# Super-blocks of 16,384 keys, one V buffer with 64 KB rows, and V products 512 columns wide in a decode-attention kernel

## The chip, the cores and the metric

The kernel runs on one core of a Trainium2 chip. The core's engines work side by side, each through its own list of instructions: TensorE (PE; its weight loads are listed apart as PEld), VectorE (DVE), ScalarE (ACT), GpSimd (POOL) and SyncE (SP, which here only issues transfers). Sixteen DMA engines move data from device memory into on-chip memory. The metric is the device time of one execution in microseconds (us).

## The reference

The result mixes two branches for a single token of width 448: `g * a + (1 - g) * b`, where g is a sigmoid of a dot product. Branch b is a small mixer MLP. Branch a, nearly all of the work, is attention of one query token over a cache of 65,536 keys, with 16 query heads that share 8 key/value heads of 256 columns:

```python
B, Sq, D = 1, 1, 448
Hq, Hkv, Sk, Dh = 16, 8, 65536, 256
q = (x @ wq).reshape(B, Sq, Hq, Dh).transpose(0, 2, 1, 3)
k = jnp.repeat(k_cache, Hq // Hkv, axis=1)
v = jnp.repeat(v_cache, Hq // Hkv, axis=1)
scores = jnp.einsum("bhqd,bhkd->bhqk", q, k) * (Dh ** -0.5)
p = softmax(scores)
o = jnp.einsum("bhqk,bhkd->bhqd", p, v)
a = o.transpose(0, 2, 1, 3).reshape(B, Sq, Hq * Dh) @ wo
```

All data are bf16. K and V are 268 MB each, and each byte is used once, for two query heads.

## The kernel before, in words

The keys are cut into 64 blocks of 8,192 (`BLK`), eight for each key/value head; n counts them. Key p·64 + j of a block lies on partition p, so one block of K or of V is a load of 4 MB with one run of 32 KB for each of 128 partitions. K has two buffers (`k_tiles`, chosen by n % 2) and V two (`v_tiles`), 128 KB per partition together.

For each block, in the order in which the loop from L442 writes it:

- 16 groups. Each group is `transposes`: eight PE transposes of 128x128 of K (L316) into PSUM and one DVE copy of 128x1024 back (L321). After every second group PE does four score products (L331), two groups behind.
- In the first block only: the issue of the load of wo (L461) and `mixer_tail`, 14 PE products (L280) that read `gel`, the mixer's activations. `gel` lies in `v_tiles[0]`, and the query weights wq lie in `v_tiles[1]`, until V needs the place.
- On SP's list: the load of V of block n (L138), then the load of K of block n + 2 (L132). The first waits until the products that read that V buffer are done, and in block 0 until `mixer_tail` has read `gel`. The second waits until the transposes of block n are done. SP executes its list strictly in order, so an issue behind a waiting one waits too.
- `max_rows`, `max_heads`, `softmax` (L355 to L396): the row maximum, its spreading over partitions by two small PE steps, the exponential on ACT, a DVE transpose of p.
- The V products of the block before (`pv`, L346): 64 products with 2 weight columns (the two query heads) and 256 moving columns, spread over four column groups of PE; the first half stands between the two PE steps of the softmax, the second half behind them. `accumulate` (L400) folds the sum into `acc`.

The V products thus run one block behind their scores. At the end of each head come `denominators`, `head_out` and `project` (L408, L420, L433). After the last block the V products of that block stand alone, then the last head's output. The last V load is cut in five pieces (`LAST`), the first K load in four (`QUARTERS`).

All instructions of one engine are chained in program order by `seq`; nothing reorders them.

Of the kernel before, what the change touches and what calls it, by code (L numbers as in the profile page):

```python
# [20 lines left out]

BLK = 8192
KP = BLK // 128


NJ = 16
NI = KP // NJ
ROWS = REP * NI


@with_exitstack
def kernel(
# [29 lines left out]
    def seq(ins):  # L62
# [17 lines left out]

    k_tiles = [kvpool.tile([128, KP, DH], BF16, name=f"kn{i}") for i in range(2)]
    v_tiles = [kvpool.tile([128, KP, DH], BF16, name=f"vt{i}") for i in range(2)]
    kT_tiles = [work.tile([128, 2, NJ, 128], BF16, name=f"kT{i}") for i in range(2)]
    p_tiles = [work.tile([128, 512], BF16, name=f"p_sb{i}") for i in range(2)]
    pT_tiles = [work.tile([128, 512], BF16, name=f"pT{i}") for i in range(2)]
    wo_sb = const.tile([128, HQ, 2, D], BF16)

    tps = [psum.tile([128, 1024], BF16, name=f"tps{i}") for i in range(3)]
    sc_ps = [psum.tile([128, 512], FP32, name=f"sc_ps{i}") for i in range(2)]
    pv_ps = psum.tile([128, DH], FP32, name="pv_ps")  # L90
    sm_ps = psum.tile([128, 512], FP32, name="sm_ps")
# [11 lines left out]
    DM = 384  # L103
    wq_m = v_tiles[1][:, 0:48, :].rearrange("p a b -> p (a b)").rearrange(
        "p (k n) -> p k n", k=3
    )
    wq_t = v_tiles[1][:, 48:56, :].rearrange("p a b -> p (a b)")

# [18 lines left out]

    def load_k(n, pieces):
        g, b = divmod(n, NB)
        src = A_k_cache[0, g, b * BLK:(b + 1) * BLK, :].rearrange("(p j) d -> p j d", j=KP)  # L130
        for j0, j1 in pieces:
            seq(nc.sync.dma_start(out=k_tiles[n % 2][:, j0:j1, :], in_=src[:, j0:j1, :]))  # L132

    def load_v(n, pieces):
        g, b = divmod(n, NB)
        src = A_v_cache[0, g, b * BLK:(b + 1) * BLK, :].rearrange("(p j) d -> p j d", j=KP)
        for j0, j1 in pieces:
            seq(nc.sync.dma_start(out=v_tiles[n % 2][:, j0:j1, :], in_=src[:, j0:j1, :]))  # L138

    WHOLE = [(0, KP)]  # L140
    QUARTERS = [(i * NJ, (i + 1) * NJ) for i in range(NI)]
    LAST = [(0, 32), (32, 48), (48, 56), (56, 60), (60, 64)]

    load_k(0, QUARTERS)
    load_k(1, WHOLE)


# [11 lines left out]
    ))  # L159
    fst = const.tile([128, REP], FP32)  # L160
    seq(nc.vector.tensor_reduce(
        out=fst[:],
        in_=ident_f[:].rearrange("p (a i r) -> p r a i", a=4, r=REP)[:, :, :, 0:1],
        op=ALU.add, axis=AXIS.XY,
    ))
    nval = const.tile([128, REP], FP32)
# [22 lines left out]
    for h in range(HQ):  # L189
# [29 lines left out]
    b1f = const.tile([128, NF], FP32)  # L219
    gel = v_tiles[0][:].rearrange("p a b -> p (a b)")[:, 0:NF * D].rearrange(  # L220
        "p (b n) -> p b n", b=NF
# [70 lines left out]

    acc = work.tile([128, DH], FP32)
    lsum = work.tile([128, 1], FP32)
# [4 lines left out]
    nb_tiles = [work.tile([128, 1], FP32, name=f"nb{i}") for i in range(2)]  # L299
    den_tiles = [work.tile([128, 1], FP32, name=f"den{i}") for i in range(2)]  # L300
    al_tiles = [work.tile([128, 1], FP32, name=f"al{i}") for i in range(3)]
    rden = work.tile([128, 1], FP32)
    esc = work.tile([128, REP], FP32)
    oT = work.tile([128, 2, REP], BF16)
# [5 lines left out]
    def transposes(n, i, c, half):  # L310

        kT = kT_tiles[(n * NI + i) % 2]
        tp = tps[state["t"] % 3]
        state["t"] += 1
        for jj in range(8):
            seq(nc.tensor.transpose(  # L316
                tp[:, jj * 128:(jj + 1) * 128],
                k_tiles[n % 2][:, i * NJ + half * 8 + jj, c * 128:(c + 1) * 128],
                ident[:, :],
            ))  # L320
        seq(nc.vector.tensor_copy(  # L321
            out=kT[:, c, half * 8:(half + 1) * 8, :],
            in_=tp[:, :].rearrange("p (j n) -> p j n", j=8),
        ))

    def scores(n, i, c):
        kT = kT_tiles[(n * NI + i) % 2]
# [12 lines left out]
    def pv(n, j0, j1):  # L340
        pT = pT_tiles[n % 2]
        vt = v_tiles[n % 2]
        for j in range(j0, j1):
            i, jj = divmod(j, NJ)
            grp = j % 4
            seq(nc.tensor.matmul(  # L346
                pv_ps[32 * grp:32 * grp + REP, :],
                lhsT=pT[:, 32 * jj + REP * i:32 * jj + REP * (i + 1)],
                rhs=vt[:, j, :],
                start=(j < 4),  # L350
                stop=(j >= KP - 4),
                tile_position=(0, 32 * grp),
            ))
# [20 lines left out]
    def softmax(n):  # L374
        b = n % NB
        nb, nb_old = nb_tiles[n % 2], nb_tiles[(n + 1) % 2]
        den, al = den_tiles[n % 2], al_tiles[n % 3]
# [8 lines left out]
        seq(nc.scalar.activation(  # L386
            out=p_tiles[n % 2][:, :], in_=sc_ps[n % 2][:, :], func=ACT.Exp, scale=scale,
            bias=nb[:, 0:1], accum_out=den[:, 0:1],
        ))
        seq(nc.vector.transpose(out=pT_tiles[n % 2][:, :], in_=p_tiles[n % 2][:, :]))  # L390
        if b > 0:
            seq(nc.vector.scalar_tensor_tensor(  # L392
                out=lsum[:], in0=lsum[:], scalar=al[:, 0:1], in1=den[:], op0=ALU.mult, op1=ALU.add
            ))
        else:
            seq(nc.vector.tensor_copy(out=lsum[:], in_=den[:]))  # L396

    def accumulate(n):
        if n % NB > 0:
            seq(nc.vector.scalar_tensor_tensor(  # L400
                out=acc[:], in0=acc[:], scalar=al_tiles[n % 3][:, 0:1], in1=pv_ps[:, :],
                op0=ALU.mult, op1=ALU.add,
            ))
        else:
            seq(nc.vector.tensor_copy(out=acc[:], in_=pv_ps[:, :]))

# [10 lines left out]
    def head_out():  # L417

        for c in range(2):
            seq(nc.tensor.matmul(  # L420
                hd_ps[:, 464 + REP * c:464 + REP * (c + 1)],
                lhsT=acc[:].rearrange("p (d c) -> p c d", c=2)[:, c, :], rhs=esc[:],
                start=True, stop=True,
            ))
# [16 lines left out]

    for n in range(NBLK):  # L442
        groups = [(i, c, half) for i in range(NI) for c in range(2) for half in range(2)]
        due = []
        head_done = n >= 2 and (n - 1) % NB == 0
        for t, (i, c, half) in enumerate(groups):
            transposes(n, i, c, half)
            if due and due[0][0] <= t:
                scores(n, *due.pop(0)[1])
            if half == 1:  # L450
                due.append((t + 2, (i, c)))
            if head_done:
                if t == 1:
                    head_out()
                if t == 3:
                    project((n - 1) // NB - 1)
        while due:
            scores(n, *due.pop(0)[1])

        if n == 0:  # L460
# [3 lines left out]
            mixer_tail()  # L464
        load_v(n, WHOLE if n < NBLK - 1 else LAST)
        if n + 2 < NBLK:
            load_k(n + 2, WHOLE)
        max_rows(n)
        if n > 0:
            pv(n - 1, 0, 32)  # L470
        max_heads(n)
        if n > 0:
            pv(n - 1, 32, KP)
        softmax(n)
        if n > 0:
            accumulate(n - 1)
        if n % NB == NB - 1 or (n == NBLK - 1):
            denominators()
    n = NBLK - 1
    pv(n, 0, KP)  # L480
    accumulate(n)
    head_out()
    project(HKV - 1)
    fin = const.tile([1, D], FP32)
# [35 lines left out]
```

## Time and profile before

| | us |
|---|---|
| median of 3 runs | 1303.34 |
| lowest and highest run | 1302.52, 1304.71 |
| span of the profiled execution (first to last instruction) | 1300.9 |
| PE busy, DVE busy, ACT busy in it | 970.5, 835.7, 73.5 |
| DVE copies of transposed K (L321), 1,024 of them | 666.9 |
| K transposes on PE (L316), 8,192 | 629.1 |
| score products (L331), 2,048 | 212.9 |
| V products (L346), 4,096 | 135.2 |
| PE idle until a K load has landed | 203.6 |

For the profiled execution only the span is recorded; it stands 2.4 us below the median of the runs. The span is read from the profile's page, which also gives the busy share of each engine and of the DMA engines in 40 equal slices of 32.5 us. The DMA queues moved 546.40 MB at a mean of 420 GB/s. A row of a group names the line, the engine, the operation and its tiles, the count, the busy time and the mean duration of one instruction in ns, and then the idle time ahead of it with what ended it. Busy times of PE overlap where four column groups work at once.

### The profile page before, as it was taken

To read this page: it belongs to the slowest core of one execution; us is meant where nothing else is said; L and a number is where in the kernel's file an instruction comes from. 1 tells how busy PE (TensorE), PEld (TensorE's weight loads), DVE (VectorE), ACT (ScalarE), POOL (GpSimd) and SP (SyncE) were. 2 spreads that over 40 slices of the span, in tenths; PEclk is the share of its full clock that TensorE was granted. 3 is DMA by queue.
4 is the path that set the end of the run, shared out by engine and by line. 5 is a ranking of instruction groups with operands and counts; after the bars stand their busy time and mean duration, and the time that the engine had idled before them with its cause. 6 is when DMAs were issued, how large, how long until landed. Compare 5 with 4: busy or idle time off the path is not lost.

```text
span 1300.9 us, 32264 instructions
## 1 busy us (share of the span) xinstructions
PE 970.5 (75%) x14750; PEld 723.8 (56%) x14750; DVE 835.7 (64%) x1599; ACT 73.5 (6%) x203; POOL 2.4 (0%) x7
## 2 busy tenths in 40 slices
PE   3876877777886877867768768778678787777786
PEld 2565655555664655655545546556556555555564
DVE  3665766766765757756757667567567566666675
ACT  4000000000000000000000000000000000000000
POOL 0000000000000000000000000000000000000000
PEclk9888888888988879889989898899888988988888
DMA  8999999999999999999999999999999999999995
GB/s 337 410 431 431 427 431 428 430 429 431 430 424 431 431 431 429 428 428 432 430 425 431 432 428 429 429 417 430 431 423 425 425 428 426 423 425 427 428 423 221
DMA packets 22830, 546.40 MB, mean 420 GB/s; under 512 B 2980, under 2 KB 5158, under 8 KB 5670
## 3 DMA queue, kind: packets, MB, share of 16 engines
q1 hardware_dynamic: 21810, 544.22, 98.1%
q8 instruction: 115, 1.88, 0.6%
q10 hardware_dynamic: 884, 0.13, 0.1%
q14 instruction: 21, 0.17, 0.0%
HBM read 544.34 MB, written 0.00 MB: 418 GB/s over the span
## 4 chain that ended last, share of the span: by engine, by line
DMA 66%; PE 31%; DVE 1%; ACT 1%; issue 0%; ACTq 0%; DVEq 0%
DMA kn<-in_A_k_cache_dram 66%; PE tps L316 24%; PE sc_ps L331 5%; DMA xt<-in_A_x_dram 1%; ACT vt L245 1%; PE hd_ps L433 1%; PE hd_ps L420 0%; PE pv_ps L346 0%; DVE kT L321 0%; PE hd_ps L280 0%; DVE pT L390 0%; DVE rmax L356 0%; ACT L256 0%; ACT p_sb L386 0%; ACTq L515 0%
## 5 line engine op out<-in xcount | busy, mean ns | idle before, releaser
L321 DVE COPY kT<-tps 128x1024 bf16<-128x1024 bf16 x1024 | 666.9, 686 | 248.0 <-PE tps L316 233.8
L316 PE MATMUL tps<-ident,kn 128*128 128x128 bf16 x8192 | 629.1, 240 | 208.7 <-DMA kn<-in_A_k_cache_dram 203.6
L316 PEld LDWEIGHTS <-kn 128*128 128x128 bf16 x8192 | 546.7, 109 | 322.4 <-DMA kn<-in_A_k_cache_dram 220.8
L331 PE MATMUL sc_ps<-kT,qpad 128*32 128x512 bf16 x2048 | 212.9, 406 | 38.6 <-DVE kT L321 38.0
L346 PE MATMUL pv_ps<-vt,pT 128*2 128x256 bf16 x4096 | 135.2, 274 | 0.0
L331 PEld LDWEIGHTS <-qpad 128*32 128x32 bf16 x2048 | 53.0, 93 | 109.3 <-issue 60.6
L346 PEld LDWEIGHTS <-pT 128*2 128x2 bf16 x4096 | 85.8, 83 | 20.3
L390 DVE STREAM_TRANSPOSE pT<-p_sb 128x512 bf16<-128x512 bf16 x64 | 45.5, 711 | 64.8 <-ACT p_sb L386 64.8
L383 ACT ACTIVATE al<-nb,nb 128x1 f32<-128x1 f32 x56 | 16.5, 295 | 1053.6 <-DVE nb L378 1053.6
L356 DVE TENSOR_REDUCE rmax<-sc_ps 128x1 f32<-128x512 f32 x64 | 44.2, 691 | 31.5 <-PE sc_ps L331 31.5
L359 PE MATMUL sm_ps<-ident_f,rmax 128*1 128x128 f32 x64 | 17.3, 270 | 52.5 <-DVE rmax L356 52.5
L386 ACT ACTIVATE p_sb<-sc_ps,nb 128x512 bf16<-128x512 f32 x64 | 42.9, 670 | 150.5 <-DVE nb L378 150.5
L378 DVE CUSTOM_DVE_ANT_0 junk<-sm_ps,nval 128x2 f32<-128x2 f32 x64 | 10.2, 159 | 59.8 <-PE sm_ps L370 59.8
L359 PEld LDWEIGHTS sm_ps<-ident_f,rmax 128*1 128x1 f32 x64 | 5.1, 79 | 71.7 <-DVE rmax L356 71.7
L400 DVE SCALAR_TENSOR_TENSOR acc<-acc,al,pv_ps 128x256 f32<-128x256 f32 x56 | 26.5, 473 | 1.5 <-PE pv_ps L346 1.5
L370 PEld LDWEIGHTS sm_ps<-mrun,ones_row 1*128 1x128 f32 x128 | 18.7, 183 | 14.6 <-issue 14.1
L370 PE MATMUL sm_ps<-mrun,ones_row 1*128 1x2 f32 x128 | 24.2, 257 | 0.3 <-DVE mrun L363 0.3
L363 DVE TENSOR_REDUCE mnew<-sm_ps 1x2 f32<-1x32 f32 x56 | 10.0, 178 | 20.3 <-PE sm_ps L359 20.3
L194 PE MATMUL hd_ps<-xm,vt 128*128 128x1 bf16 x96 | 3.6, 165 | 12.2 <-DMA xm<-in_A_x_dram 12.2
L386 ACT ACTIVATION_READ_ACCUMULATOR p_sb<-sc_ps,nb 128x1 f32 x64 | 12.2, 191 | 0.0
L194 PEld LDWEIGHTS <-vt 128*128 128x128 bf16 x96 | 3.6, 104 | 12.1 <-DMA vt<-in_A_wq_dram 11.8
L392 DVE SCALAR_TENSOR_TENSOR lsum<-lsum,al,den 128x1 f32<-128x1 f32 x56 | 9.9, 177 | 0.0
(66 smaller groups left out, 96.9 us busy)
## 6 DMA issues: line engine op xcount, KB each, us to landing
kn<-in_A_k_cache_dram SPq DMA_DIRECT2D x63, 4096.0 KB, 27.7
vt<-in_A_v_cache_dram SPq DMA_DIRECT2D x63, 4096.0 KB, 32.4
kn<-in_A_k_cache_dram SPq DMA_DIRECT2D x4, 1024.0 KB, 11.8
wo_sb<-in_A_wo_dram SPq DMA_DIRECT2D x1, 3584.0 KB
vt<-in_A_wq_dram SPq DMA_DIRECT2D x1, 3072.0 KB
vt<-in_A_v_cache_dram SPq DMA_DIRECT2D x1, 2048.0 KB, 20.8
vt<-in_A_v_cache_dram SPq DMA_DIRECT2D x1, 1024.0 KB
vt<-in_A_wq_dram SPq DMA_DIRECT2D x2, 256.0 KB, 3.9
```

Of the source, the lines that this page charges most:

```text
L245: seq(nc.scalar.activation(out=gel[:, b, :], in_=h_bc[:], func=ACT.Gelu_apprx_tanh, scale=w1f[:, b:b + 1], bias=b1f[:, b:b + 1],))
L316: seq(nc.tensor.transpose(tp[:, jj * 128:(jj + 1) * 128], k_tiles[n % 2][:, i * NJ + half * 8 + jj, c * 128:(c + 1) * 128], ident[:, :],))
L321: seq(nc.vector.tensor_copy(out=kT[:, c, half * 8:(half + 1) * 8, :], in_=tp[:, :].rearrange("p (j n) -> p j n", j=8),))
L331: seq(nc.tensor.matmul(S[32 * a:32 * (a + 1), :], lhsT=qpad[:, c, g, i, :], rhs=kT[:, c, :, 32 * a:32 * (a + 1)], start=(i == 0 and c == 0 ...
L346: seq(nc.tensor.matmul(pv_ps[32 * grp:32 * grp + REP, :], lhsT=pT[:, 32 * jj + REP * i:32 * jj + REP * (i + 1)], rhs=vt[:, j, :], start=(j ...
L356: seq(nc.vector.tensor_reduce(out=rmax[:], in_=sc_ps[n % 2][:, :], op=ALU.max, axis=AXIS.X))
L359: seq(nc.tensor.transpose(sm_ps[0:1, 0:128], rmax[:, 0:1], ident_f[:, :]))
L370: seq(nc.tensor.matmul(sm_ps[:, 128:128 + REP], lhsT=ones_row[0:1, :], rhs=mrun[0:1, :], start=True, stop=True))
L383: seq(nc.scalar.activation(out=al[:], in_=nb_old[:], func=ACT.Exp, scale=-1.0, bias=nb[:, 0:1]))
L386: seq(nc.scalar.activation(out=p_tiles[n % 2][:, :], in_=sc_ps[n % 2][:, :], func=ACT.Exp, scale=scale, bias=nb[:, 0:1], accum_out=den[:, ...
L390: seq(nc.vector.transpose(out=pT_tiles[n % 2][:, :], in_=p_tiles[n % 2][:, :]))
L400: seq(nc.vector.scalar_tensor_tensor(out=acc[:], in0=acc[:], scalar=al_tiles[n % 3][:, 0:1], in1=pv_ps[:, :], op0=ALU.mult, op1=ALU.add,))
```

## The change

`BLK` becomes 16,384, so a head has four super-blocks and the kernel 32. Key p·128 + j of a super-block lies on partition p. K is loaded in two halves of 4 MB (64 of the 128 key columns each, 32 KB runs at a pitch of 64 KB), one into each K buffer. V is one load of 8 MB in rows of 64 KB into a single buffer `vt`, which takes the place of the two V buffers; wq and `gel` lie in that buffer before. A super-block has 32 groups and one softmax over a 128x512 tile of scores, in which 16 of each 32 rows now hold scores and 8 did before. The V products take two groups of columns at once: 4 weight columns, 512 moving columns, 64 products for a super-block; only the diagonal half of each result is used, and `fst` and `esc` pick it in `head_out`, which has twice as many products. The V products are no longer one block behind: they stand behind the softmax of their own super-block. SP's list is V(n), then the first and the second K half of n + 1. The first K load is cut in two pieces; the last V load is cut in five.

The core of the diff:

```diff
-BLK = 8192
-KP = BLK // 128
+BLK = 16384
+VP = BLK // 128
+KP = VP // 2
-NI = KP // NJ
+NI = VP // NJ
-    v_tiles = [kvpool.tile([128, KP, DH], BF16, name=f"vt{i}") for i in range(2)]
+    vt = kvpool.tile([128, VP, DH], BF16, name="vt")
-    pv_ps = psum.tile([128, DH], FP32, name="pv_ps")
+    pv_ps = psum.tile([128, 2, DH], FP32, name="pv_ps")
-    wq_m = v_tiles[1][:, 0:48, :].rearrange("p a b -> p (a b)").rearrange(
+    wq_m = vt[:, 0:48, :].rearrange("p a b -> p (a b)").rearrange(
-    wq_t = v_tiles[1][:, 48:56, :].rearrange("p a b -> p (a b)")
+    wq_t = vt[:, 48:56, :].rearrange("p a b -> p (a b)")
+    def load_v(n):
+        seq(nc.sync.dma_start(out=vt[:, :, :], in_=v_src(n)))
+    def load_v_last(n):
+        for j0, j1 in ((0, 64), (64, 96)):
+            seq(nc.sync.dma_start(out=vt[:, j0:j1, :], in_=v_src(n)[:, j0:j1, :]))
+        for j0, j1 in ((0, 8), (8, 12), (12, 16)):
...
-    load_k(0, QUARTERS)
-    load_k(1, WHOLE)
+    load_k(0, 0, [(0, 32), (32, KP)])
+    load_k(0, 1, WHOLE)
-    gel = v_tiles[0][:].rearrange("p a b -> p (a b)")[:, 0:NF * D].rearrange(
+    gel = vt[:, 56:128, :].rearrange("p a b -> p (a b)")[:, 0:NF * D].rearrange(
+    def pv(ip, j0, j1):
+        for jj in range(j0, j1):
+            grp = jj % 4
             seq(nc.tensor.matmul(
+                pv_ps[32 * grp:32 * grp + 2 * REP, :, :],
+                lhsT=pT[:, 32 * jj + 2 * REP * ip:32 * jj + 2 * REP * (ip + 1)],
+                rhs=vt[:, 2 * ip * NJ:2 * (ip + 1) * NJ, :].rearrange(
+                    "p (i j) d -> p i j d", i=2
+                )[:, :, jj, :],
...
         if n == 0:
...
             mixer_tail()
-        load_v(n, WHOLE if n < NBLK - 1 else LAST)
-        if n + 2 < NBLK:
-            load_k(n + 2, WHOLE)
+        if n < NBLK - 1:
+            load_v(n)
+            load_k(n + 1, 0, WHOLE)
+            load_k(n + 1, 1, WHOLE)
+        else:
+            load_v_last(n)
         max_rows(n)
-        if n > 0:
-            pv(n - 1, 0, 32)
         max_heads(n)
-        if n > 0:
-            pv(n - 1, 32, KP)
         softmax(n)
-        if n > 0:
-            accumulate(n - 1)
-        if n % NB == NB - 1 or (n == NBLK - 1):
+        if n % NB == NB - 1:
             denominators()
-    n = NBLK - 1
-    pv(n, 0, KP)
-    accumulate(n)
-    head_out()
-    project(HKV - 1)
+        for ip in range(NI // 2):
+            pv(ip, 0, NJ)
+        accumulate(n)
+        if n % NB == NB - 1:
+            head_out()
+            project(n // NB)
```

More of the change, by code (lines that the diff above doesn't have):

```diff
@@ L18 @@
 REP = HQ // HKV
-BLK = 8192
-KP = BLK // 128
+BLK = 16384
+VP = BLK // 128
+KP = VP // 2
 NJ = 16
-NI = KP // NJ
-ROWS = REP * NI
+NI = VP // NJ
 @with_exitstack
@@ L81 @@
     k_tiles = [kvpool.tile([128, KP, DH], BF16, name=f"kn{i}") for i in range(2)]
-    v_tiles = [kvpool.tile([128, KP, DH], BF16, name=f"vt{i}") for i in range(2)]
+    vt = kvpool.tile([128, VP, DH], BF16, name="vt")
     kT_tiles = [work.tile([128, 2, NJ, 128], BF16, name=f"kT{i}") for i in range(2)]
-    p_tiles = [work.tile([128, 512], BF16, name=f"p_sb{i}") for i in range(2)]
-    pT_tiles = [work.tile([128, 512], BF16, name=f"pT{i}") for i in range(2)]
+    p_sb = work.tile([128, 512], BF16)
+    pT = work.tile([128, 512], BF16)
     wo_sb = const.tile([128, HQ, 2, D], BF16)
@@ L126, with load_k, v_src @@
         seq(nc.scalar.dma_start(out=b2b[:], in_=B_b2.rearrange("(o n) -> o n", o=1)))
-    def load_k(n, pieces):
+    def load_k(n, h, pieces):
         g, b = divmod(n, NB)
-        src = A_k_cache[0, g, b * BLK:(b + 1) * BLK, :].rearrange("(p j) d -> p j d", j=KP)
+        src = A_k_cache[0, g, b * BLK:(b + 1) * BLK, :].rearrange("(p j) d -> p j d", j=VP)
         for j0, j1 in pieces:
-            seq(nc.sync.dma_start(out=k_tiles[n % 2][:, j0:j1, :], in_=src[:, j0:j1, :]))
-    def load_v(n, pieces):
+            seq(nc.sync.dma_start(
+                out=k_tiles[h][:, j0:j1, :], in_=src[:, h * KP + j0:h * KP + j1, :]
+            ))
+    def v_src(n):
         g, b = divmod(n, NB)
-        src = A_v_cache[0, g, b * BLK:(b + 1) * BLK, :].rearrange("(p j) d -> p j d", j=KP)
-        for j0, j1 in pieces:
-            seq(nc.sync.dma_start(out=v_tiles[n % 2][:, j0:j1, :], in_=src[:, j0:j1, :]))
+        return A_v_cache[0, g, b * BLK:(b + 1) * BLK, :].rearrange("(p j) d -> p j d", j=VP)
+    def load_v(n):
[4 more added lines that the diff above has]
+        for j0, j1 in ((0, 8), (8, 12), (12, 16)):
+            seq(nc.sync.dma_start(
+                out=vt[:, 96:128, :].rearrange("p (i j) d -> p i j d", i=2)[:, :, j0:j1, :],
+                in_=v_src(n)[:, 96:128, :].rearrange("p (i j) d -> p i j d", i=2)[:, :, j0:j1, :],
+            ))
     WHOLE = [(0, KP)]
-    QUARTERS = [(i * NJ, (i + 1) * NJ) for i in range(NI)]
-    LAST = [(0, 32), (32, 48), (48, 56), (56, 60), (60, 64)]
-    load_k(0, QUARTERS)
-    load_k(1, WHOLE)
+    load_k(0, 0, [(0, 32), (32, KP)])
+    load_k(0, 1, WHOLE)
     ident = const.tile([128, 128], BF16)
@@ L159 @@
     ))
[L160 to L165, printed above, removed]
+    fst = const.tile([128, 2, REP], FP32)
+    for e in range(2):
+        seq(nc.vector.tensor_reduce(
+            out=fst[:, e, :],
+            in_=ident_f[:].rearrange("p (a i r) -> p r a i", a=4, r=REP)[:, :, :, e:e + 1],
+            op=ALU.add, axis=AXIS.XY,
+        ))
     nval = const.tile([128, REP], FP32)
@@ L290, in mixer_tail @@
         seq(nc.vector.tensor_tensor(out=rest[:], in0=y_sb[:], in1=rest[:], op=ALU.subtract))
-    acc = work.tile([128, DH], FP32)
+    acc = work.tile([128, 2, DH], FP32)
     lsum = work.tile([128, 1], FP32)
@@ L299 @@
     nb_tiles = [work.tile([128, 1], FP32, name=f"nb{i}") for i in range(2)]
-    den_tiles = [work.tile([128, 1], FP32, name=f"den{i}") for i in range(2)]
-    al_tiles = [work.tile([128, 1], FP32, name=f"al{i}") for i in range(3)]
+    den = work.tile([128, 1], FP32)
+    al = work.tile([128, 1], FP32)
     rden = work.tile([128, 1], FP32)
-    esc = work.tile([128, REP], FP32)
+    esc = work.tile([128, 2, REP], FP32)
     oT = work.tile([128, 2, REP], BF16)
@@ L310, in transposes @@
     def transposes(n, i, c, half):
-        kT = kT_tiles[(n * NI + i) % 2]
+        kT = kT_tiles[i % 2]
         tp = tps[state["t"] % 3]
@@ L317, in transposes @@
                 tp[:, jj * 128:(jj + 1) * 128],
-                k_tiles[n % 2][:, i * NJ + half * 8 + jj, c * 128:(c + 1) * 128],
+                k_tiles[i // (NI // 2)][:, i % (NI // 2) * NJ + half * 8 + jj, c * 128:(c + 1) * 128],
                 ident[:, :],
@@ L326, in scores @@
     def scores(n, i, c):
-        kT = kT_tiles[(n * NI + i) % 2]
+        kT = kT_tiles[i % 2]
         S = sc_ps[n % 2]
@@ L338, in scores @@
             ))
[L340 to L351, printed above, removed]
+    def pv(ip, j0, j1):
+        for jj in range(j0, j1):
+            grp = jj % 4
+            seq(nc.tensor.matmul(
+                pv_ps[32 * grp:32 * grp + 2 * REP, :, :],
[3 more added lines that the diff above has]
+                )[:, :, jj, :],
+                start=(ip == 0 and jj < 4),
+                stop=(ip == NI // 2 - 1 and jj >= NJ - 4),
                 tile_position=(0, 32 * grp),
@@ L376, in softmax @@
         nb, nb_old = nb_tiles[n % 2], nb_tiles[(n + 1) % 2]
-        den, al = den_tiles[n % 2], al_tiles[n % 3]
         seq(nc.vector.tensor_tensor_reduce(
@@ L386, in softmax @@
         seq(nc.scalar.activation(
-            out=p_tiles[n % 2][:, :], in_=sc_ps[n % 2][:, :], func=ACT.Exp, scale=scale,
+            out=p_sb[:, :], in_=sc_ps[n % 2][:, :], func=ACT.Exp, scale=scale,
             bias=nb[:, 0:1], accum_out=den[:, 0:1],
         ))
-        seq(nc.vector.transpose(out=pT_tiles[n % 2][:, :], in_=p_tiles[n % 2][:, :]))
+        seq(nc.vector.transpose(out=pT[:, :], in_=p_sb[:, :]))
         if b > 0:
@@ L400, in accumulate @@
             seq(nc.vector.scalar_tensor_tensor(
-                out=acc[:], in0=acc[:], scalar=al_tiles[n % 3][:, 0:1], in1=pv_ps[:, :],
+                out=acc[:], in0=acc[:], scalar=al[:, 0:1], in1=pv_ps[:, :, :],
                 op0=ALU.mult, op1=ALU.add,
@@ L404, in accumulate @@
         else:
-            seq(nc.vector.tensor_copy(out=acc[:], in_=pv_ps[:, :]))
+            seq(nc.vector.tensor_copy(out=acc[:], in_=pv_ps[:, :, :]))
     def denominators():
@@ L419, in head_out @@
         for c in range(2):
[L420 to L424, printed above, removed]
+            for e in range(2):
+                seq(nc.tensor.matmul(
+                    hd_ps[:, 464 + REP * c:464 + REP * (c + 1)],
+                    lhsT=acc[:, e, :].rearrange("p (d c) -> p c d", c=2)[:, c, :],
+                    rhs=esc[:, e, :],
+                    start=(e == 0), stop=(e == 1),
+                ))
         seq(nc.vector.tensor_copy(
@@ L442 @@
     for n in range(NBLK):
+        due = []
         groups = [(i, c, half) for i in range(NI) for c in range(2) for half in range(2)]
-        due = []
-        head_done = n >= 2 and (n - 1) % NB == 0
         for t, (i, c, half) in enumerate(groups):
@@ L451 @@
                 due.append((t + 2, (i, c)))
-            if head_done:
-                if t == 1:
-                    head_out()
-                if t == 3:
-                    project((n - 1) // NB - 1)
         while due:
@@ L464 @@
             mixer_tail()
-        load_v(n, WHOLE if n < NBLK - 1 else LAST)
-        if n + 2 < NBLK:
-            load_k(n + 2, WHOLE)
+        if n < NBLK - 1:
[4 more added lines that the diff above has]
+            load_v_last(n)
         max_rows(n)
-        if n > 0:
-            pv(n - 1, 0, 32)
         max_heads(n)
-        if n > 0:
-            pv(n - 1, 32, KP)
         softmax(n)
-        if n > 0:
-            accumulate(n - 1)
-        if n % NB == NB - 1 or (n == NBLK - 1):
+        if n % NB == NB - 1:
             denominators()
-    n = NBLK - 1
-    pv(n, 0, KP)
-    accumulate(n)
-    head_out()
-    project(HKV - 1)
+        for ip in range(NI // 2):
[4 more added lines that the diff above has]
+            project(n // NB)
     fin = const.tile([1, D], FP32)
```

## The prediction

> **What bounds the kernel now.** I first read the rows of DMA traffic on the page, then its queues.
>
> ```profile
> DMA  8999999999999999999999999999999999999995
> GB/s 337 410 431 431 427 431 428 430 429 431 430 424 431 431 431 429 428 428 432 430 425 431 432 428 429 429 417 430 431 423 425 425 428 426 423 425 427 428 423 221
> ...
> q1 hardware_dynamic: 21810, 544.22, 98.1%
> q8 instruction: 115, 1.88, 0.6%
> ```
>
> From the third slice to the last but one the 16 engines are never idle, at 417 to 432 GB/s, and SP's queue q1 (the loads) fills 98.1% of 16 engines' span. The load stream sets the time: only what changes its rate, stops it, or lies before its first or behind its last byte can move the end. Next, whether the queue ever runs short, by the DMA issues, and whether the compute engines keep up, by the groups.
>
> ```profile
> kn<-in_A_k_cache_dram SPq DMA_DIRECT2D x63, 4096.0 KB, 27.7
> vt<-in_A_v_cache_dram SPq DMA_DIRECT2D x63, 4096.0 KB, 32.4
> L321 DVE COPY kT<-tps 128x1024 bf16<-128x1024 bf16 x1024 | 666.9, 686 | 248.0 <-PE tps L316 233.8
> L316 PE MATMUL tps<-ident,kn 128*128 128x128 bf16 x8192 | 629.1, 240 | 208.7 <-DMA kn<-in_A_k_cache_dram 203.6
> ```
>
> A 4 MB load takes 4.194 MB / 429 GB/s = 9.8 us and lands 27.7 us after its issue, so some 18 us of work stand ahead of it. PE waits 203.6 us in all for K: compute has slack. Then the two ends of the span. The start, by the timeline:
>
> ```profile
> 17.12 0.61 SPq L461 DMA_DIRECT2D wo_sb<-in_A_wo_dram  x1
> ...
> 40.80 2.81 PE L280 MATMUL hd_ps<-vt,w2b 128*1 128x448 bf16 x14
> 43.64 0.34 SPq L138 DMA_DIRECT2D vt<-in_A_v_cache_dram  x1
> ```
>
> SP issues everything up to wo by 17.7 us and then stands until `mixer_tail` (L280) has read `gel`; V(0) goes out at 43.64. The end, by the busy time of stages (stage; length; PE, PEld, DVE, ACT, POOL; clock; DMA share; GB/s):
>
> ```profile
> 1275.00:1280.00 5.00, 5.00 (x47) 4.33 (x45) 3.35 (x5) 0.00 (x0) 0.00 (x0) 0.50 1.01 424
> 1280.00:1285.00 5.00, 5.00 (x77) 3.62 (x75) 4.57 (x8) 0.00 (x0) 0.00 (x0) 0.99 0.54 230
> 1285.00:1290.00 5.00, 3.60 (x71) 2.32 (x68) 3.69 (x8) 0.00 (x0) 0.00 (x0) 1.00 0.49 200
> 1290.00:1295.00 5.00, 3.83 (x112) 2.76 (x100) 1.77 (x7) 0.96 (x3) 0.00 (x0) 1.00 0.21 78
> ```
>
> At 1280 half of the DMA engines are through; the other half, some 12 us behind, finish near 1292. And by the chain that ended last, merged in order of time:
>
> ```profile
> 1274.27 3.60 PE tps L316 x32
> ...
> 1293.05 1.95 PE pv_ps L346 x64
> 1295.02 0.49 DVE acc L400
> ```
>
> The last K block lands at 1274.2; from there to 1300.9, 26.7 us, are compute: 14.0 of transposes and scores, 4.8 of softmax and denominators, 1.95 of V products, the rest head output and the store.
>
> **Part 1, the start: one V buffer, with `gel` in it.** V(0) is still behind `mixer_tail`, but block 0 now has 32 groups, not 16. The second half follows without a pause (its K, the old block 1, was there: PE began on that at 46.94 without a wait for it). In steady rows of the timeline PE starts a new pair of groups each 1.33 us (35.92, 37.25, 38.58), the time of two DVE copies of 0.66, so 8 x 1.33 = 10.6 us, and V(0) is issued at 43.64 + 10.6 = 54.3. From an issue to moving bytes takes about 1.5 us (the load issued at 12.18 shows a DMA share of 0.02 in 12 to 13 and 0.41 in 13 to 14). So V(0) moves from 55.8. The queue is empty before that: wo is the stretch at about 380 GB/s that begins at 36; 3.67 MB / 380 GB/s = 9.7 us, with the laggards 46 to 47.5. SP's next two K loads stand behind V(0), though the first K buffer was free at 41. The engines idle 55.8 - 46.3 = **9.5 us** (8 if the laggards count). If the added half ran at the low clock (0.58 between 30 and 35, where a pair takes 2.36 us), four pairs at that pace add 4: 14 is the upper end. I take 9.5, since PE runs on without the pauses after which the low clock shows. As the stream bounds the rest, all of it reaches the end.
>
> **Part 2, the steady state: nothing.** Let T be the landing of a first K half. Second half T+9.8, V T+29.4, next K T+39.1. Compute: first half 13.9 (with the slow clock after a pause, as from 1274.3), second 10.6, so T+24.5; softmax 4.3 (1288.2 to 1292.5) less 0.55 for the V products that stood in it, T+28.3; V is there at T+29.4; products 2 x 1.95 = 3.9, T+33.3. PE then waits 5.8 us. On SP's list the K halves can be issued at T+13.9 and T+24.5, V at T+33.3; their turns in the stream come at T+29.4, T+39.1, T+48.9; with 1.5 of latency the margins are 13 to 14 us. So the lost overlap of V products and softmax, and the lost second V buffer, are hidden by PE's 5.8 us; if that cover were gone, each us would cost 31, once for each super-block. The halved softmax work (32 x about 3 us of DVE and ACT) is in the slack too and earns nothing.
>
> Against this stands a rule of the Trainium skill (Trainium Kernel Development and Optimization, Best Practices): double-buffer, so that loads overlap compute. By it, V with one buffer would expose its products, 3.9 us, 31 times: 121 us. The trace's 27.7 us to landing is the counter-row: the two K buffers in the queue cover the V buffer's turn. Only at the start, where nothing stands behind wo, does the rule bite.
>
> **Part 3, V in rows of 64 KB.** The trace's packet records give a median of 309, 611 and 1215 ns for packets of 8, 16 and 32 KB: twice 611 less 1215 is 7 ns of fixed cost. V falls from 512 packets an engine to 256: -256 x 7 ns = **-1.8 us**. It is 0 if rows are still split at 32 KB. A loss from the doubled pitch (64 KB) is not excluded by any row; equal transfers differ from slice to slice by 423 against 429 GB/s, and 1.4% of the V half would be +9 us. I take -1.8, since 8 KB runs at a pitch of 32 KB (first K pieces) moved at the fixed-cost line.
>
> The Trainium skill (DMA: Bandwidth & Descriptors, Anatomy of one DMA) fits a transfer issued by GpSimd with 2.0 us plus a term in bytes. By that 32 fewer V loads would save 64 us; the DMA share of 1.00 over stretches of 300 us says that queued loads don't pay it here (100 to 400 us, one of four such stages: 429 GB/s).
>
> **Part 4, fewer instructions to fetch.** 2,048 products and as many weight loads go, and 32 softmaxes of 17 instructions: 4,600 of 32,264, so 16 of 115 fetches of 16 KB on the same engines. At 611 ns each, over the half of the engines that lags, **-1.2 us** (over all 16, -0.6). The lag of 12 us fits 115 x 0.6 / 8 = 9.
>
> **Part 5, the end.** The last super-block's second K half again lands 8 MB before the stream's end. From that landing: scores end 24.5 - 9.8 = 14.7 later (+0.7); no V products inside the softmax (-0.5); 64 products of 512 columns for 64 of 256: 3.9 for 1.95 (+1.95; bounds 3.4 at exact column time, 5.3 at the 0.33 us that four score products of 512 columns take); `accumulate` over 512 columns (+0.4 of 0.49); head output with eight products for four (+0.6 of 0.65). **+3.2 us**, 2.6 to 4.6. V's last piece is there about 19.5 after the landing, the products end after 22.9: V stays hidden.
>
> **Sum.** 9.5 + 3.2 - 1.8 - 1.2 = +9.7 us. The span 1300.9 becomes 1310.6; on the median 1303.34 (2.4 above) it is **1313 us**. Set-up edits (a wider `qpad`, its seven copies, a second `fst`) end before the DVE wait for ACT's `ez` at 27.6 and cost nothing; each us beyond that would.
>
> **Rivals.**
> - Starved stream (0.05): PE's chain outgrows 39.1 us a super-block. For: PE, DVE and ACT now stand in a row at each softmax. Against: 5.8 us of slack. At 40 us it costs 31 x 0.9 = 28: 1341.
> - Pitch (0.04): V and K at 64 KB pitch move 1.4% slower; twice 9 us on top: 1331.
> - Faster (0.04): long rows speed up the stream by more than the 12.7 us of the start and end. Place: V's 256 packets an engine. It decides from (12.7 - 1.2) / 256 = 45 ns saved for each 64 KB, against 7 seen; at 70 ns the sum is 12.7 - 17.9 - 1.2 = -6.4: 1297.
> - Even (0.04): the gap shrinks to some 1.5 us, because V(0) is let out earlier or wo takes longer: 1.5 + 3.2 - 3.0 = +1.7, 1305.
> - It doesn't do what it says: 64 KB rows are split in two, so part 3 is 0: 1315. It lies in the forecast's own range.
>
> **Chances.** Forecast 0.83, from 8 + 2.6 - 3.0 = +7.6 (1311) to 14 + 4.6 - 0.6 = +18 (1321); with the run spread and part of the even case below, and 1 us above, the range is 1308 to 1322. Faster by over 0.2% (2.6 us, about what a measurement here can tell) 0.04, within it 0.04, slower 0.92.
>
> **What would show it.** Timeline: V(0) issued near 54, DMA share near 0 from 47.5 to 55.8. Stages of 300 us still at DMA share 1.00 and 428 to 430 GB/s; V packets halved if rows go out whole; about 99 instruction packets; PE's wait for K about 6 us a super-block. Wrong: stages at a lower rate without idle (pitch), idle DMA in mid-span (starving), a V(0) issue well before 54.

## The result, and the profile after

The changed kernel takes 1311.04 us (median of 4 runs, 1309.25 to 1312.02); the kernel before, measured with it, 1302.93 (4 runs). The ratio is 1.0058, 95% interval 1.0045 to 1.0071: 8.1 us slower, where 9.7 were forecast and 1308 to 1322 was the range. The profiled execution took 1309.25 us, the shortest of the four, with a span of 1307.5, so the profile explains 6.6 of the 8.1 us; the other spans are 1308.0 to 1310.2.

The DMA rows of the page after, to be held against those of before:

```profile
DMA  8799999999999999999999999999999999999994
GB/s 332 315 416 429 431 432 437 430 430 427 425 431 430 440 428 425 427 430 437 432 433 421 431 430 431 429 432 419 429 428 434 423 415 437 425 424 439 421 423 202
...
q1 hardware_dynamic: 17298, 544.22, 97.3%
q8 instruction: 98, 1.61, 0.5%
```

The second slice has fallen from 410 to 315 GB/s; between the third slice and the last the rates lie at 415 to 440 GB/s, for 417 to 432 before. q1 (SP's loads) moves the same bytes in 17,298 packets for 21,810: the rows of V went out whole. Instruction packets (q8) are 98 for 115. The start, by SP's timeline and then by stages of 1 us (length, PE, PEld, DVE, ACT, POOL, clock, DMA share, GB/s):

```profile
53.50 0.33 SPq L141 DMA_DIRECT2D vt<-in_A_v_cache_dram  x1
```

```profile
45.00:46.00 1.00, 1.00 (x18) 0.67 (x16) 0.96 (x3) 0.00 (x0) 0.00 (x0) 1.00 0.85 300
46.00:47.00 1.00, 1.00 (x20) 0.78 (x17) 0.96 (x2) 0.00 (x0) 0.00 (x0) 1.00 0.34 131
47.00:48.00 1.00, 1.00 (x20) 0.89 (x16) 0.96 (x3) 0.00 (x0) 0.00 (x0) 1.00 0.08 30
48.00:49.00 1.00, 1.00 (x18) 0.67 (x16) 1.00 (x2) 0.00 (x0) 0.00 (x0) 1.00 0.00 0
...
53.00:54.00 1.00, 0.47 (x3) 0.01 (x1) 0.50 (x1) 0.00 (x0) 0.00 (x0) 1.00 0.00 0
54.00:55.00 1.00, 0.00 (x0) 0.00 (x0) 0.93 (x3) 0.00 (x0) 0.00 (x0) 1.00 3.00 983
```

V(0) is issued at 53.50 (forecast 54.3; before 43.64), and by the packet records the engines stand still from about 46.2 to 54.6, 8.4 us (forecast 9.5). A packet counts in the slice in which it begins, so the 3.00 is fifteen packets of 64 KB that begin within 0.3 us. In mid-span, by stages of 300 us:

```profile
100.00:400.00 300.00, 228.66 (x2946) 151.33 (x2942) 178.48 (x309) 7.32 (x22) 0.00 (x0) 0.85 1.00 430
400.00:700.00 300.00, 230.30 (x3060) 155.84 (x3060) 187.74 (x323) 6.54 (x20) 0.00 (x0) 0.87 1.00 431
700.00:1000.00 300.00, 226.80 (x2917) 152.66 (x2917) 175.73 (x302) 7.31 (x22) 0.00 (x0) 0.84 1.00 429
```

The stream does not pause there: 430, 431, 429 GB/s for 429, 429, 428 before. PE's waits for loads (engine, what it waited for, us in total, times, longest):

```profile
PE pv_ps L356 <- DMA vt<-in_A_v_cache_dram: 122.6, 29, 18.2
PE tps L328 <- DMA kn<-in_A_k_cache_dram: 105.6, 29, 5.6
```

That is 3.8 us for V and 3.3 for K in a super-block, 7.1 together. The longest wait for V, 18.2 us, is the one in super-block 0. The end, by the chain that ended last:

```profile
1290.16 0.42 PE sc_ps L343 x4
...
1295.03 5.27 PE pv_ps L356 x64
1300.33 0.76 DVE acc L411
1301.13 1.12 PE hd_ps L432 x8
```

The last V products take 5.27 us, 1.95 before and 3.9 in the forecast. The first half of the last K lands at 1267.1, so the second about 9.8 later, at 1276.9 (its last completion mark in the trace stands at 1276.8), against 1274.2 for the last K before: the stream is 2.7 us late. From there to the end it is 30.6 us for 26.7: 3.9 us more of compute. 2.7 + 3.9 = 6.6, for these two executions.

### The profile page after: what moved, and what is told of

Same layout as the page of the kernel before. It is cut to its first block, busy times and chain, and to the rows that moved or that the text cites. A ratio compares the mean times of both kernels' runs of the same rounds, so it can differ in the third digit from the quotient of the medians.

```text
span 1307.5 us, 27867 instructions
## 1 busy us (share of the span) xinstructions
PE 969.1 (74%) x12638; PEld 651.2 (50%) x12638; DVE 769.2 (59%) x1348; ACT 42.7 (3%) x107; POOL 4.2 (0%) x7
## 3 DMA queue, kind: packets, MB, share of 16 engines
q1 hardware_dynamic: 17298, 544.22, 97.3%
## 4 chain that ended last, share of the span: by engine, by line
DMA 69%; PE 28%; DVE 1%; ACT 1%; issue 0%; ACTq 0%; DVEq 0%
DMA kn<-in_A_k_cache_dram 38%; DMA vt<-in_A_v_cache_dram 30%; PE tps L328 17%; PE pv_ps L356 6%; PE sc_ps L343 4%; DMA xt<-in_A_x_dram 1%; ACT vt L257 1%; PE hd_ps L446 0%; PE hd_ps L432 0%; DVE kT L333 0%; PE hd_ps L292 0%; DVE acc L411 0%; DVE pT L401 0%; DVE rmax L368 0%; ACT L268 0%
## 5 line engine op out<-in xcount | busy, mean ns | idle before, releaser
L328 PE MATMUL tps<-ident,kn 128*128 128x128 bf16 x8192 | 588.6, 230 | 108.0 <-DMA kn<-in_A_k_cache_dram 105.6
L328 PEld LDWEIGHTS <-kn 128*128 128x128 bf16 x8192 | 504.1, 104 | 229.8 <-DMA kn<-in_A_k_cache_dram 121.8
L356 PE MATMUL pv_ps<-vt,pT 128*4 128x512 bf16 x2048 | 184.5, 539 | 122.6 <-DMA vt<-in_A_v_cache_dram 122.6
L356 PEld LDWEIGHTS <-pT 128*4 128x4 bf16 x2048 | 61.6, 111 | 231.8 <-issue 168.3
L411 DVE SCALAR_TENSOR_TENSOR acc<-acc,al,pv_ps 128x512 f32<-128x512 f32 x24 | 17.9, 747 | 170.1 <-PE pv_ps L356 170.1
L401 DVE STREAM_TRANSPOSE pT<-p_sb 128x512 bf16<-128x512 bf16 x32 | 22.8, 711 | 32.8 <-ACT p_sb L397 32.8
L394 ACT ACTIVATE al<-nb,nb 128x1 f32<-128x1 f32 x24 | 7.1, 294 | 945.0 <-DVE nb L389 945.0
L368 DVE TENSOR_REDUCE rmax<-sc_ps 128x1 f32<-128x512 f32 x32 | 22.1, 691 | 15.5 <-PE sc_ps L343 15.5
L397 ACT ACTIVATE p_sb<-sc_ps,nb 128x512 bf16<-128x512 f32 x32 | 21.5, 673 | 291.7 <-DVE nb L389 291.7
L382 PE MATMUL sm_ps<-mrun,ones_row 1*128 1x2 f32 x64 | 14.1, 287 | 14.1 <-DVE mrun L381 11.7
L432 PEld LDWEIGHTS hd_ps<-esc,acc 128*128 128x128 f32 x64 | 8.1, 196 | 10.9 <-DVE acc L411 10.9
```

The lines of the kernel that those rows point to most:

```text
L328: seq(nc.tensor.transpose(tp[:, jj * 128:(jj + 1) * 128], k_tiles[i // (NI // 2)][:, i % (NI // 2) * NJ + half * 8 + jj, c * 128:(c + 1) * ...
L356: seq(nc.tensor.matmul(pv_ps[32 * grp:32 * grp + 2 * REP, :, :], lhsT=pT[:, 32 * jj + 2 * REP * ip:32 * jj + 2 * REP * (ip + 1)], rhs=vt[: ...
L368: seq(nc.vector.tensor_reduce(out=rmax[:], in_=sc_ps[n % 2][:, :], op=ALU.max, axis=AXIS.X))
L382: seq(nc.tensor.matmul(sm_ps[:, 128:128 + REP], lhsT=ones_row[0:1, :], rhs=mrun[0:1, :], start=True, stop=True))
L397: seq(nc.scalar.activation(out=p_sb[:, :], in_=sc_ps[n % 2][:, :], func=ACT.Exp, scale=scale, bias=nb[:, 0:1], accum_out=den[:, 0:1],))
L401: seq(nc.vector.transpose(out=pT[:, :], in_=p_sb[:, :]))
```

## The experiments

All are short edits, and all times are compared with runs of the kernel before on the same chip.

**The gap closed: a1_tail_early.** In the loop of super-block 0:

```diff
             transposes(n, i, c, half)
+            if n == 0 and t == 15:
+                seq(nc.sync.dma_start(out=wo_sb[:], in_=...))
+                mixer_tail()
...
-        if n == 0:
-            seq(nc.sync.dma_start(out=wo_sb[:], in_=...))
-            mixer_tail()
```

> The changed kernel with one edit: the issue of wo and the 14 mixer products stand after the first 16 groups of super-block 0 instead of after all 32. Theory (gap): most of the added time is the idle stream ahead of V(0). V(0) goes out near 43.6 us instead of 53.5, the DMA share no longer falls to 0 between 47 and 54, and the time falls by 7 to 9 us from 1311.0, to 1302 to 1304, within 0.2% of before. Rival (stream): the single V buffer, the 64 KB pitch or the serial softmax slow the stream itself in mid-span; then the gap closes and the time stays above 1308.

1302.01 us for 1302.08 (ratio 0.9996, 0.9987 to 1.0005). V(0) goes out at 41.68:

```profile
41.68 0.33 SPq L141 DMA_DIRECT2D vt<-in_A_v_cache_dram  x1
```

The share of the DMA engines no longer falls (stages of 1 us, last two columns):

```profile
46.00:47.00 1.00, 1.00 (x18) 0.71 (x16) 1.00 (x2) 0.00 (x0) 0.00 (x0) 1.00 0.83 339
47.00:48.00 1.00, 1.00 (x18) 0.67 (x16) 1.00 (x3) 0.00 (x0) 0.00 (x0) 1.00 1.72 741
```

The gap is the cost: with it closed, the difference from before is gone, although one V buffer, wide rows and wide products remain. The same kernel once more, as a base for later runs:

> The kernel of a1_tail_early once more, as the base for the two others: equal to before within 0.2%, 1301 to 1303.

1301.95 us for 1302.25 (0.9994, 0.9985 to 1.0003).

The end of the stream in a1_tail_early, by the same stages as before:

```profile
1280.00:1285.00 5.00, 1.89 (x21) 0.92 (x17) 2.57 (x8) 0.93 (x3) 0.00 (x0) 1.00 0.54 215
1285.00:1290.00 5.00, 4.07 (x38) 1.70 (x42) 1.21 (x4) 0.03 (x1) 0.00 (x0) 0.51 0.21 81
```

A share of 0.21 stood at 1290 to 1295 before. Without the gap the changed stream is through 5 us earlier than the old one; a longer compute tail (the clock of 0.51 in the second line belongs to it) takes that back. The completion marks say the same: the last K half is there at 1269.5, 4.7 us earlier than before, and from there to the end it is 30.8 us for 26.7. So a1 equals before by two differences that cancel.

**The gap put into the kernel before: b1_gap_in_before.**

```diff
+            if n == 1 and t == 5:
+                mixer_tail()
+                load_v(0, WHOLE)
+                load_k(2, WHOLE)
...
-            mixer_tail()
-        load_v(n, WHOLE if n < NBLK - 1 else LAST)
+        if n > 0:
+            load_v(n, WHOLE if n < NBLK - 1 else LAST)
...
```

> The kernel before with one edit: the mixer products, V(0) and K(2) stand behind the sixth group of block 1 instead of behind block 0, so that V(0) is let out near 53 us as in the changed kernel, with blocks of 8,192, two V buffers and narrow products as they were. Theory (gap): the stream is idle from about 46.3 to 54.5 and the time rises by 8 us, to 1310. Rival (the gap is absorbed, because the stream has room to catch up): it stays within 1 us of before.

1307.01 us for 1302.46 (1.0036, 1.0022 to 1.0050): 4.6 us more. V(0) was let out at 50.09, earlier than meant:

```profile
50.09 0.34 SPq L138 DMA_DIRECT2D vt<-in_A_v_cache_dram  x1
```

```profile
46.00:47.00 1.00, 1.00 (x18) 0.77 (x18) 1.00 (x3) 0.00 (x0) 0.00 (x0) 1.00 0.18 68
...
50.00:51.00 1.00, 1.00 (x17) 0.80 (x16) 0.87 (x2) 0.00 (x0) 0.00 (x0) 1.00 0.00 0
51.00:52.00 1.00, 1.00 (x17) 0.67 (x15) 0.97 (x3) 0.00 (x0) 0.00 (x0) 1.00 1.98 524
```

By the packet records the 16 engines were idle here for 5.4 us on average; by the same count it is 8.3 us in the changed kernel. 5.4 us idle cost 4.6, nearly one to one. The expectation of 8 had reckoned with an issue near 53. Absorption is refuted: the 1,250 us that follow win back little of it (the interval of the rise is 2.9 to 6.5 us).

**V in rows of 32 KB: a2_v_two_loads.**

```diff
-        seq(nc.sync.dma_start(out=vt[:, :, :], in_=v_src(n)))
+        for j0 in (0, KP):
+            seq(nc.sync.dma_start(
+                out=vt[:, j0:j0 + KP, :], in_=v_src(n)[:, j0:j0 + KP, :]))
```

> As a1, and each 8 MB V load is issued as two loads of 4 MB, rows of 32 KB at a pitch of 64 KB. Theory (fixed cost): a 64 KB packet took 2420 ns, two of 32 KB 2 x 1215 = 2430, so 256 packets more for each engine cost 256 x 10 ns = 2.6 us against a1. Rival (pitch or size of a row slows the stream): the time falls against a1. Rival (row length inert): equal to a1 within 1 us, with V packets still at the same rate.

1303.58 us for 1302.08 (1.0005, 0.9997 to 1.0014): 1.2 us over a1 by the ratios, 1.6 by the medians, and the intervals overlap. The sign is the expected one, half the size; that it is not nothing is not shown by the times. The packet records show it in the stream: the packets of q1 took 1275.4 us of each engine's time (mean of the 16) for 1272.6 in a1, 2.8 us more, near the 2.6 expected. That the pitch of 64 KB slows the stream is refuted: the 32 KB packets of K took a median of 1215 ns at either pitch.

**More instructions: a3, a5, p1, p2.** a3_pv_256 halves the width of the V products and doubles their number:

```diff
...
-                pv_ps[32 * grp:32 * grp + 2 * REP, :, :],
...
+            for e in range(2):
+                seq(nc.tensor.matmul(
+                    pv_ps[32 * grp:32 * grp + 2 * REP, e, :],
...
+                    rhs=vt[:, (2 * ip + e) * NJ + jj, :],
...
```

> As a1, and each V product of 512 columns is done as two of 256: 4,096 V products as before the change, with 4 weight columns. Theory (fetches): 4,096 instructions more need about 15 more instruction fetches on the lagging half of the DMA engines, 12 us / 115 = 0.1 us each on the end, so +1.5 us, and at the low clock of the last super-block 128 products take 5.8 for 5.3, +0.5: together +2 against a1. Rival (width of the products is inert): equal to a1 within 0.6 us.

1304.39 us for 1302.08 (1.0016, 1.0007 to 1.0025), 2.6 us over a1 by the ratios, with 114 instruction packets for 98. a5_64_idle_steps has as many packets and leaves the V products as in a1; `idle(m)` is m transposes of the identity that nobody reads:

```diff
             pv(ip, 0, NJ)
+        if n < NBLK - 1:
+            idle(64)
```

> As a1_tail_early, and in all super-blocks but the last PE does 64 idle transposes behind the V products, whose results nobody reads: 3,968 instructions more, 4.3 to 6 us of PE a super-block, less than the 6.9 us that PE waits there for V and K. Theory (fetches): they need 15 more instruction fetches, which lengthen the lagging half of the DMA engines as in a3, and the time rises by 1.5 to 2.5 us over a1. Rival (width): a3 rose because products of 256 columns are dearer, not for its instructions; then a5 is equal to a1 within 0.7 us. Rival (starved stream): PE's added work reaches the stream, and the time rises by 30 us or more.

1303.11 us for 1302.46 (1.0003, 0.9994 to 1.0012), 0.9 over a1, 114 packets. It lies between the two expectations and decides nothing, except that 64 steps do not starve the stream. p1_pool_fetches was to bring more packets without PE:

```diff
+    spare = const.tile([1, 1], FP32)
...
+        if 0 < n < NBLK - 1:
+            for _ in range(300):
+                seq(nc.gpsimd.memset(spare[:], 0.0))
```

> As a1_tail_early, and GpSimd, which is idle, runs 9,000 one-element memsets that nobody reads, with no wait to or from another engine. Theory (fetches): 9,000 instructions more are 32 to 36 instruction packets of 16 KB more; at 1.05 us each on the lagging eight DMA engines that is 4.2 to 4.7 us of lag, and the time rises by 3 to 5 us over a1. Rival (fetches are inert, and a3 rose by the width of its products): the packets are there, and the time stays within 1 us of a1.

1329.22 us for 1302.25 (1.0207, 1.0193 to 1.0221). The experiment failed by its design: 9,000 memsets at 147 ns each make 1,321 us, so GpSimd itself ended last, by the head of its chain:

```profile
POOL spare L459 68%; POOL qpad L191 0%; POOL ident masks.py:199 0%; POOLq L524 0%; POOL ident masks.py:197 0%; POOLq L513 0%
```

Its packets also came on another queue (q14, 90 for 21). p2_one_column_steps puts 160 products of one column where a5 has its idle steps:

```diff
+            for _ in range(160):
+                seq(nc.tensor.matmul(sm_ps[:, 200:201], lhsT=ident[:, :],
+                    rhs=ident[:, 0:1], start=True, stop=True))
```

> As a1_tail_early, and in all super-blocks but the last PE does 160 products of one column behind the V products, which nobody reads: 9,920 instructions more, some 27 ns for a product with its weight load by the wq products of the start, 4.3 us a super-block, inside PE's wait of 6.9. Theory (fetches): 36 to 39 instruction packets more on q8, at 1.05 us each on the lagging eight DMA engines 4.7 to 5.1 us of lag, so the lag at the end grows from 8 to 10 us to 13 to 15 and the time rises by 3 to 5 us over a1. Rival (fetches inert): the packets are there and the time stays within 1 us of a1.

1309.23 us for 1302.00 (1.0051, 1.0037 to 1.0065), 7.2 us over a1 by the ratios, more than expected. Its packets, and the end of its stream:

```profile
q8 instruction: 137, 2.24, 0.7%
```

```profile
1280.00:1285.00 5.00, 5.00 (x78) 3.77 (x77) 4.84 (x9) 0.00 (x0) 0.00 (x0) 1.00 1.02 416
1285.00:1290.00 5.00, 4.71 (x72) 3.33 (x69) 4.88 (x8) 0.00 (x0) 0.00 (x0) 1.00 0.55 228
```

In a1 the share fell to 0.54 one stage earlier, at 1280. So the half of the engines that finishes first is late too, and the lag has not grown: the sixteen completion marks of the last K half are 10.7 us apart in p2, 10.2 in a1_tail_early and 11.2 in a1_again (15.4 for the last K load before; a load marks its completion sixteen times). The picture of the expectation, that only the lagging half pays, has fallen. That more PE instructions cost time here is shown at 39 packets (0.18 us each), consistent at 16 (0.16 in a3, 0.06 in a5). The packet records give a part of the cause (us of each engine's time, mean of the 16; the rise over a1_tail_early by the ratios of the runs):

| | instruction packets (q8) | their time | time of the loads (q1) | rise in time |
|---|---|---|---|---|
| a1_tail_early | 98 | 6.4 | 1272.6 | |
| a3_pv_256 | 114 | 7.5 | 1273.9 | 2.6 |
| a5_64_idle_steps | 114 | 7.5 | 1272.9 | 0.9 |
| p2_one_column_steps | 137 | 8.9 | 1275.7 | 7.2 |

a1_again has 6.5 and 1272.1, so half a microsecond is the scatter of one kernel. In p2 the instruction packets themselves took 2.5 us more, and the load packets 3.1 more. What lengthened the loads, the packets beside them or the extra PE work, stays open. A stream starved by PE is not the main part, although PE's wait for V in p2 was down to 68.5 us: between 70 and 1260 us the engines were idle for 2.8 us on average, for 2.0 and 1.1 in the two runs of a1.

**How much PE work fits: a6_160_idle_steps.** As a5 with 160 steps.

> As a5 with 160 idle transposes: 10.7 us at the full clock, up to 13 with some at the low one, 4 to 6 us above PE's slack of 6.9. Theory (slack): PE now bounds each super-block, the stream runs dry once in each, and the time rises by 31 times the excess, 110 to 190 us over a1, with a DMA share below 1.00 in the stages of 300 us. Rival (the single V buffer leaves more room than PE's slack, 13 us of issue margin): the rise stays under 10 us.

1354.03 us for 1302.46 (1.0394, 1.0375 to 1.0413): 52 us over a1, 1.7 for each of 31 super-blocks. PE's waits for V are gone but for one, and no wait for K is left among the longest rows; first a1_tail_early, then a6:

```profile
PE pv_ps L356 <- DMA vt<-in_A_v_cache_dram: 115.6, 29, 13.5
PE tps L328 <- DMA kn<-in_A_k_cache_dram: 107.0, 29, 6.1
```

```profile
PE pv_ps L356 <- DMA vt<-in_A_v_cache_dram: 12.1, 1, 12.1
```

```profile
400.00:700.00 300.00, 272.16 (x4069) 204.47 (x4061) 166.39 (x291) 6.55 (x20) 0.00 (x0) 0.94 0.99 415
```

The starved stream exists, and PE's slack is where it begins, not the 13 us of issue margin. The size was off: the 160 steps took 9.1 us in a super-block looked at (645.71 to 654.82), not 10.7 to 13. A step took 57 ns where the expectation had 67 at the full clock, and it had added up to 2.3 us for steps at the low clock, while PE was granted 0.94 there. 9.1 - 1.7 = 7.4 us of slack, close to the 6.9 of the waits.

**The clock at the end: a4_pe_kept_busy.** On a1, in the last super-block only:

```diff
+        if n == NBLK - 1:
+            warm(8)
         max_rows(n)
         max_heads(n)
+        if n == NBLK - 1:
+            warm(32)
```

`warm(m)` is m transposes of the identity into PSUM that nobody reads.

> As a1, and in the last super-block PE does 8 idle transposes of the identity ahead of the softmax's first PE step and 32 behind its second, whose results nobody reads. Theory (clock): the last 64 V products took 5.27 us because PE had paused and was granted 0.66 of its clock; kept busy it is granted 1.0 and they take 3.4 to 3.9, so the end comes about 1.5 us earlier than in a1. Rival (width): products of 512 columns take 82 ns each whatever the clock; they stay at 5.3 and the time is equal to a1 or later.

1298.99 us for 1302.08 (0.9972, 0.9961 to 0.9984), 3 us under a1. The last V products in the chain, of a1_tail_early and of a4:

```profile
1286.52 6.29 PE pv_ps L356 x48
...
1295.00 1.33 PE hd_ps L446 x4
```

```profile
1285.88 3.58 PE pv_ps L356 x64
...
1291.65 0.93 PE hd_ps L453 x4
```

(The chain counts 48 in a1; the timeline has all 64, in 6.33 us.) In this execution of a1 the clock was low from 1285.14 to 1291.96, for most of the products, so a4 gains 2.7 us on the products and 0.4 on the last step, not the 1.5 estimated from the changed kernel, where the clock had come back after 3.4 of the 5.27 us. The low stretch is not equally long in every execution: in a1_again it ended at 1289.19, after 3.4 us, and the products took 4.99:

```profile
1286.39 4.99 PE pv_ps L356 x61
```

Beside that execution a4 gains 1.4 us on the products; how the 3 us between the medians divide is known for single executions only. The stage of the products in a1_tail_early and in a4 (PE and PEld busy, clock in the third column from the end):

```profile
1286.40:1290.00 3.60, 3.60 (x37) 1.23 (x41) 0.40 (x2) 0.00 (x0) 0.00 (x0) 0.50 0.12 45
```

```profile
1285.80:1289.50 3.70, 3.64 (x65) 1.45 (x64) 0.40 (x3) 0.00 (x0) 0.00 (x0) 1.00 0.07 24
```

Width is refuted as the cause: at the full clock a product of 512 columns takes 56 ns (3.58 / 64), and at the low one about 107 (in a1_tail_early the weight loads of four products follow each other every 0.43 us).

**Awake at both ends: c1_awake_at_both_ends.** a4 and, behind the V products of the last super-block but one, `warm(64)`.

> As a4_pe_kept_busy, and PE also does 64 idle transposes behind the V products of the last super-block but one, so that it is awake when the last K lands. Theory (clock): the first 32 transposes of the last super-block took 3.1 us at the low clock and take 2.0, the following 16 gain some tenths, and the end comes another 1.0 to 1.5 us earlier than in a4, until V's last piece, which lands at about the time of the last products, is what ends last: 1297.5 to 1298.5, 0.3 to 0.4% below before. Rival (V's last piece already ends the chain): equal to a4 within 0.5 us.

1298.84 us for 1302.25 (0.9974, 0.9964 to 0.9984), equal to a4. The rival holds: the chain of c1 runs over V, not K.

```profile
1254.61 34.60 DMA vt<-in_A_v_cache_dram
1289.21 0.04 issue
1289.25 0.42 PE pv_ps L356 x4
```

The last four products wait for V's last piece, so quicker scores buy nothing further. a4 and c1 are the versions that beat both kernels, by 0.3% against before.

## Why the prediction was right, point by point

1. **The bound** is right. A pause of the stream reaches the end: closing it takes 8.1 us off by the ratios (1.0058 to 0.9996), putting one of 5.4 us into the old kernel costs 4.6.
2. **Part 1, the gap**: 9.5 forecast; 8.4 measured, for V(0) was issued 0.8 us earlier than forecast and began to move about 1 us after its issue, not 1.5. This is the step that decides the sign, and it is shown from both sides.
3. **Part 2, nothing in mid-span**: right for the stream, 429 to 431 GB/s. PE's waits are 7.1 us a super-block where the forecast's times give 6.9, but they divide otherwise: 3.8 for V (1.1 forecast) and 3.3 for K (5.8, and "about 6" among the signs). One cause is the V products: 5.51 us in the super-block at 666, at a clock of 0.65, where 3.9 were reckoned. PE had enough slack all the same. The Trainium skill's rule to double-buffer (Trainium Kernel Development and Optimization, Best Practices) was weighed at 121 us in the forecast. a1 has one V buffer and a ratio of 0.9996: here the rule bites only where no other load stands in the queue, at the start.
4. **Part 3, long rows**: -1.8 forecast. The packets went out whole, with a median of 2420 ns for 64 KB against 2 x 1215, so 10 ns for each, -2.6 us by these medians. All packets of q1 together took 1272.4 us of each engine's time for 1275.7 before, -3.3, with K's and the last pieces in it; by a2's time V's rows give 1.2 to 1.6, with overlapping intervals.
5. **Part 4, fetches**: 98 packets (99 forecast), and q8 took 6.5 us of each engine's time for 7.6, about the -1.2 forecast. That is luck: such a packet took a median of 1073 ns in the kernel before, not 611, and its time is here spread over all 16 engines, not over the half that lags; the two errors cancel. If p2's 0.18 us held for 17 packets, the gain would be 3 us by estimate; that is not shown.
6. **Part 5, the end**: +3.2 forecast, +3.9 in the profile. The mis-sized term is the V products: 3.9 forecast from two times the old 1.95, 5.27 measured, 6.29 in a1. The old row had been taken at the full clock; the change moved the products behind a pause. Softmax (-0.4), `accumulate` (+0.3) and head output (+0.5) came nearly as forecast, the scores 1.0 earlier, and the store of the result took 0.5 longer, which was not forecast.

The errors lean against each other: the stream was 2.7 us late in the profile where 6.5 were forecast (the gap 1.1 smaller, the gains of parts 3 and 4 by the packet records 4.5 for 3.0; 1.2 us are not accounted for), and the compute tail longer by 0.7. The medians differ by 8.1 and not by the profile's 6.6, so these parts are known to 1 or 2 us only. That the total came near the 9.7 is partly luck; that the gap makes most of it is shown.

## What to carry to other kernels

When a double buffer becomes a single one, look for the place where no other load is queued, here the start, before fearing the steady state: 31 of 32 super-blocks hid it, and the first cost 8 us. What lives in a buffer ahead of its real use (here `gel`) decides when the first load may leave; moving the reader forward by 16 groups was worth 8 to 9 us. And a duration taken from a row belongs to the clock of that row: work that is moved behind a pause must be priced by the clock that is granted there.

## What the runs showed of the hardware

- PE's granted clock fell to 0.50 behind a softmax in which PE did three short steps (0.27, 0.38, 0.38 us) in 4.4 us, the longest pause 2.2 us. It came back after 3.4 us of work in the changed kernel (low from 1295.02 to 1298.43), but in a1_tail_early only after 5.5 us of V products without a pause (1286.45 to 1291.96). The changed kernel:

```profile
1295.00:1298.00 3.00, 3.00 (x33) 1.07 (x36) 0.40 (x2) 0.00 (x0) 0.00 (x0) 0.50 0.12 46
1298.00:1300.40 2.40, 2.27 (x40) 0.76 (x32) 0.07 (x1) 0.00 (x0) 0.00 (x0) 0.91 0.00 0
```

The Trainium skill (TensorE: Matmul & The Clock Gate, Part 1: The HAM clock gate) gives some 3.4 us both for the idle window that lowers the clock and for the busy one that restores it. The return in the changed kernel agrees, that in a1_tail_early took longer; the fall came here without an entirely idle stretch of that length.
- About four thousand more PE instructions came with 0.9 us more (a5, within the noise) or 2.6 (a3), and nearly ten thousand with 7.2 (p2), while the loads moved at a DMA share of 1.00.
- The sixteen completion marks of one load drift apart during the run: in the kernel before they are 6.6 us apart at 305 us and 15.4 for the last K load; in the changed kernel 10.8 for the last K half. Neither 16 nor 39 more instruction packets widened this (11.1 in a3, 10.9 in a5, 10.7 in p2, for 10.2 and 11.2 in the two runs of a1).
- Beside GpSimd's 9,000 one-element memsets the load stream ran at 421, 420 and 418 GB/s in the stages from 400 us on, where a1 had 429, 427 and 428; this was not followed up.
